# Attention ahead of two MoE layers: the mask added in PSUM by TensorE, one wide maximum and one wide sum per group, exps from PSUM, v sums on GpSimd, first weights loaded later

## Chip, core and metric

One core of one Trainium2 chip runs the whole program in one launch. The metric is device time in microseconds (us) of that core. The kernel before takes 1644.41 us (median of 3 runs, 1643.33 to 1644.82).

## What is computed

```python
# attention: B=2, H=8, S=768, D=64, block 32, window 16, nb = 24
k_sum = k.reshape(B, H, nb, block, D).max(axis=3)
v_sum = v.reshape(B, H, nb, block, D).mean(axis=3)
scores_l = where(|i - j| < 16, scale * q @ k.T, -1e9)          # scale = 1/8
scores_s = scale * q @ k_sum.T + log(32)
a = softmax(concat([scores_l, scores_s]))                      # sum + 1e-9 below the line
x = a @ concat([v, v_sum])                                     # -> [1536, 512]
# layer 1: 4 experts of 512 -> 1024 -> 512, all tokens, weighted by given probabilities
# layer 2: 8 experts of the same size, weighted by 8 rounds of row and column scaling of exp(logits)
```

All in float32 in and out.

## The kernel before

**Attention** runs over 8 pairs of heads (`pairs`), each in 3 groups (`NG`) of 4 query tiles of 64 rows (`GT`, `QT`). A query tile of both heads makes 128 rows; each row has 120 scores (`KX`): a band of 96 keys and the 24 block maxima of k. For a pair, `prep_k` transposes k and takes block maxima, `prep_q` transposes q into the block-diagonal tile `bd`, `reduce_v` sums v over 8 neighbouring rows (`vr`), `prep_v` finishes that sum with a matmul (`pv`, `vb`), and `spread_v` copies the 24 block means to the 24 last partitions of `vs`, whose first 96 partitions `load_vs` fills.

A group goes through `s1` (scores, mask, row maximum `nm`), `s1b` (exp, sum `sm`, reciprocal, and the multiply L404 on GpSimd), `s2` (transpose) and `s3` (times v). The loop at L445 has 24 + 4 passes; pass w, called **window w** here, issues s3 of group w-4, s2 of w-3, s1b of w-1, s1 of w, then, by w modulo 3, `prep_k` (0) or `prep_q` (1) of the next pair. `vslot` sets the sums of v at windows 0, 2, 4, 7, 10, 13, 16, 19; `prep_v` follows one window later, `spread_v` two. The schedule is manual: each engine and SyncE's DMA queue work in the order of the code.

At the end of each window `filler` issues work for the first layer: at window 3 the loads of the first weights (`load_w2(0)`, `load_w1(0)`, 512 KB each), from window 5 one piece per window of their split into a rounded high part (VectorE) and a rest (GpSimd, L128, and sums of quarters L178), from window 9 pieces that split x in the same way, from window 20 one step of the first products (`early`) per window.

**The MoE layers** follow as 48 units of weights (expert, quarter) times 2 halves of the tokens: TensorE makes products of the split parts (L487) and the second matmul (L562 to L564), the other engines split weights and add.

PSUM has 5 buffers of tag "m" (`ps`, `pa`, `po`, `pz`, `pm`) and 3 of tag "x".

## Time and profile before

| | |
|---|---|
| median of 3 runs | 1644.41 us (1643.33 to 1644.82) |
| the profiled execution | 1645.07 us, span 1643.4 us |
| busy, share of the span | PE 97%, PEld 87%, DVE 56%, ACT 36%, POOL 34% |
| chain that ended last | PE 90%, DVE 6%, ACT 1%, others 3% |

PE is TensorE's matmuls, PEld its weight loads, DVE is VectorE, ACT ScalarE, POOL GpSimd, SPq SyncE's DMA queue. The profile cuts the span in 40 slices of 41 us; attention fills about the first three. Windows are found on VectorE by their first instruction, L402 (it belongs to the sum of the group before).

### The profile page before, as it was taken

The page shows a single profiled execution, that of the slowest core. Times are in us where ns is not written, and L with a number is a line of the kernel's source. Part 1 is how long each engine was busy: PE and PEld are TensorE (multiplying, and loading weights), DVE is VectorE, ACT ScalarE, POOL GpSimd, SP SyncE. Part 2 cuts the span into 40 slices and gives each one's busy share as a digit, 9 for nine tenths or more (in the row PEclk, how much of TensorE's full clock was granted, in tenths as well). Part 3 has the DMA queues.
Part 4 walks back from the last instruction along what each step waited for, and adds up shares of the span by engine and source line. Part 5 has one row for each costly group of instructions (what it writes and reads, how often), then busy time and mean ns, then how long its engine had stood idle before and what let it go on. Part 6 is the DMA issues. An engine that isn't in the chain of part 4 may idle for free.

```text
span 1643.4 us, 21876 instructions
## 1 busy us (share of the span) xinstructions
PE 1599.0 (97%) x8419; PEld 1437.7 (87%) x8419; DVE 922.3 (56%) x1711; ACT 586.5 (36%) x1369; POOL 558.3 (34%) x642
## 2 busy tenths in 40 slices
PE   6879999999999999999999999999999999999999
PEld 5768899899899987889998998998998999989987
DVE  6886554554554556675555555545545545555555
ACT  4763233333333335433333333323323323323321
POOL 3644333323324333424324324324323323333330
PEclk9889999999999999999999999999999999999999
DMA  9831001001001100101100100100100100100102
GB/s 185 161 83 52 26 26 52 27 26 50 28 26 40 38 1 26 53 26 41 37 27 31 47 26 27 52 26 27 52 27 27 51 26 26 52 26 26 52 0 78
DMA packets 84520, 70.26 MB, mean 43 GB/s; under 512 B 36032, under 2 KB 69056, under 8 KB 84416
## 3 DMA queue, kind: packets, MB, share of 16 engines
q1 hardware_dynamic: 84416, 68.87, 14.5%
q8 instruction: 66, 1.08, 0.3%
q14 instruction: 38, 0.31, 0.1%
HBM read 64.53 MB, written 3.15 MB: 41 GB/s over the span
## 4 chain that ended last, share of the span: by engine, by line
PE 90%; DVE 6%; ACT 1%; issue 1%; DMA 1%; POOL 0%; SPq 0%; DVEq 0%; ACTq 0%
PE px L487 35%; PE pm L564 16%; PE pm L563 16%; PE pm L562 16%; PE pz L487 6%; ACT s L398 1%; DVE scr L211 1%; DVE vr L342 1%; DVE s L388 1%; DVE sm L402 1%; PE pg L622 0%; DVE hlo_b L500 0%; DVE c L516 0%; DMA vn<-in_v_dram 0%; DMA scr<-in_moe_w_dram 0%
## 5 line engine op out<-in xcount | busy, mean ns | idle before, releaser
L582 DVE SCALAR_TENSOR_TENSOR acc<-pm,pp,acc 128x512 f32<-128x512 f32 x359 | 269.6, 751 | 195.0 <-PE pm L564 193.3
L516 DVE TENSOR_TENSOR c<-pz,c 128x384 f32<-128x384 f32 x96 | 53.4, 557 | 317.9 <-PE pz L487 317.8
L128 POOL TENSOR_TENSOR w1lo_b<-scr,w1hi_b 128x512 fp32r<-128x512 f32 (+1 forms) x144 | 116.9, 830 | 317.0 <-ACT w1hi_b L125 309.4
L128 POOL TENSOR_TENSOR w1lo_a<-scr,w1hi_a 128x512 fp32r<-128x512 f32 (+1 forms) x144 | 118.4, 841 | 305.9 <-ACT w1hi_a L125 296.0
L521 ACT COPY c<-px 128x384 f32<-128x384 f32 x96 | 46.1, 480 | 436.6 <-PE px L487 436.5
L487 PE MATMUL px<-xhi,w1hi_a 128*128 128x384 f32 x576 | 195.5, 339 | 2.0 <-ACT c L521 1.0
L487 PE MATMUL px<-xhi,w1hi_b 128*128 128x384 f32 x576 | 194.1, 337 | 0.8 <-ACT c L530 0.8
L487 PE MATMUL px<-xlo,w1hi_a 128*128 128x384 f32 x576 | 193.8, 336 | 0.2 <-POOL xlo L128 0.2
L487 PE MATMUL px<-xhi,w1lo_a 128*128 128x384 f32 x576 | 193.8, 336 | 0.0
L487 PE MATMUL px<-xhi,w1lo_b 128*128 128x384 f32 x576 | 193.3, 336 | 0.0
L487 PE MATMUL px<-xlo,w1hi_b 128*128 128x384 f32 x576 | 193.3, 336 | 0.0
L582 DVE SCALAR_TENSOR_TENSOR acc<-pm,p,acc 128x512 f32<-128x512 f32 x180 | 135.0, 751 | 97.0 <-PE pm L564 97.0
L178 POOL TENSOR_TENSOR scr<-scr 128x256 f32<-128x256 f32 x188 | 137.6, 742 | 3.7
L516 DVE TENSOR_TENSOR c<-px,c 128x384 f32<-128x384 f32 x192 | 107.0, 557 | 46.6 <-PE px L487 46.5
L128 POOL TENSOR_TENSOR w2lo_a<-scr,w2hi_a 128x512 fp32r<-128x512 f32 x48 | 61.2, 1296 | 161.8 <-ACT w2hi_a L125 159.1
L128 POOL TENSOR_TENSOR w2lo_b<-scr,w2hi_b 128x512 fp32r<-128x512 f32 x48 | 60.9, 1292 | 161.0 <-ACT w2hi_b L125 161.0
L564 PE MATMUL pm<-w2hi_b,hlo_b 128*128 128x512 f32 x288 | 113.4, 394 | 2.3 <-DVE hlo_b L500 2.3
L495 ACT ACTIVATE hhi_a<-c 128x384 fp32r<-128x384 f32 x144 | 75.6, 525 | 112.0 <-DVE c L516 112.0
L562 PE MATMUL pm<-w2hi_b,hhi_b 128*128 128x512 f32 x288 | 112.8, 391 | 0.5 <-ACT hhi_b L495 0.5
L562 PE MATMUL pm<-w2hi_a,hhi_a 128*128 128x512 f32 x288 | 112.5, 391 | 0.7 <-ACT hhi_a L495 0.7
L564 PE MATMUL pm<-w2hi_a,hlo_a 128*128 128x512 f32 x288 | 112.6, 391 | 0.5 <-DVE hlo_a L500 0.5
L495 ACT ACTIVATE hhi_b<-c 128x384 fp32r<-128x384 f32 x144 | 75.6, 525 | 104.6 <-DVE c L516 104.5
(148 smaller groups left out, 3613.0 us busy)
## 6 DMA issues: line engine op xcount, KB each, us to landing
scr<-in_moe_w_dram SPq DMA_DIRECT2D x96, 512.0 KB, 4.6
vs<-in_v_dram SPq DMA_DIRECT2D x16, 240.0 KB, 4.8
kn<-in_k_dram SPq DMA_DIRECT2D x16, 192.0 KB, 4.0
qn<-in_q_dram SPq DMA_DIRECT2D x16, 192.0 KB, 4.4
vn<-in_v_dram SPq DMA_DIRECT2D x8, 384.0 KB, 3.8
out_dram<-acc SPq DMA_DIRECT2D x12, 256.0 KB, 2.0
vs<-vb SPq DMA_DIRECT2D x8, 144.0 KB
vs<-in_v_dram SPq DMA_DIRECT2D x32, 24.0 KB, 4.5
```

What stands on the lines that cost most here:

```text
L128: lo_eng.tensor_tensor(out=lo, in0=src, in1=hi.bitcast(F32), op=ALU.subtract)
L178: sum_eng.tensor_tensor(out=st[:, o], in0=x, in1=y, op=op)
L211: sum_eng.tensor_tensor(out=out, in0=x, in1=y, op=ALU.subtract)
L342: nc.vector.tensor_reduce(out=vr[i], in_=vn[i].rearrange("x h c d -> x h d c"), axis=AX.X, op=ALU.add)
L487: nc.tensor.matmul(pm, w[l][:, a, c, :], r[:, x, :], start=first and i == 0, stop=i == n - 1, skip_group_check=True,)
L495: nc.scalar.activation(out=hhi[:, f, t * HB:(t + 1) * HB], in_=c, func=AF.Relu)
L516: nc.vector.tensor_tensor(out=c, in0=pm, in1=c, op=ALU.add)
L521: nc.scalar.copy(out=c11, in_=px)
L562: nc.tensor.matmul(pm, hhi[:, c, ts], w["w2hi"][:, c, :], start=(c == 0), stop=False)
L563: nc.tensor.matmul(pm, hhi[:, c, ts], w["w2lo"][:, c, :], start=False, stop=False)
L564: nc.tensor.matmul(pm, hlo[:, c, ts], w["w2hi"][:, c, :], start=False, stop=(c == FC - 1))
L582: nc.vector.scalar_tensor_tensor(out=acc[T], in0=pm, scalar=scal, in1=acc[T], op0=ALU.mult, op1=ALU.add)
```

## The change

1. **Mask in PSUM** (`s1`): per group, two more matmuls with an identity as weights: the mask of 4 tiles (480 columns, fp32r, starting the accumulation), and the rest of log(32) after rounding (96 columns). The four score matmuls accumulate on them. The tables `maskr`, `maskl` and `identr` are made once, at the start, on VectorE.
2. **Scale in `prep_q`**: the copies of q become multiplications by 1/8.
3. **One wide maximum**: the four custom instructions at L388 (add mask, scale, write s, minimum), each with an accumulator read, become one TENSOR_REDUCE of 480 elements out of PSUM.
4. **Exps read PSUM** (`s1b`): scores no longer go through SBUF before the exp; the accumulator reads are gone, and one TENSOR_REDUCE of 480 elements on VectorE makes the sums.
5. **v sums on GpSimd** (`reduce_v`): one TENSOR_REDUCE of 1024 elements on VectorE becomes three additions on GpSimd, of 512, 256 and 128 elements.
6. **First weights later** (`filler`): loads at window 6 instead of 3; pieces from window 8 instead of 5, two of them at windows 8, 12 and 16.

```diff
@@ -48,8 +48,7 @@
     NG = NQ // GT
     GW = GT * QT
     SC = 1.0 / math.sqrt(D)
-    NEG = -1.0e9 / SC
-    FMAX = 3.0e38
+    NEG = -float(2 ** 30)
     BLK = S
     NB = NT // BLK
     TPB = BLK // P
@@ -224,6 +223,9 @@
 
     def attention(apool, filler):
         mask = apool.tile([P, 6, KX], F32, name="mask", bufs=1)
+        maskr = apool.tile([P, 6, KX], F32R, name="maskr", bufs=1)
+        maskl = apool.tile([P, GT, NS], F32R, name="maskl", bufs=1)
+        identr = apool.tile([P, P], F32R, name="identr", bufs=1)
         sel = apool.tile([NS * VQ, NS], F32, name="sel", bufs=1)
         bd = [apool.tile([P, NQ, 2, QT], F32, name=f"bd{i}", bufs=1) for i in range(2)]
         nsc = S // P
@@ -292,7 +294,13 @@
                         base=sgn * off + WIN,
                         channel_multiplier=-sgn,
                     )
-        nc.gpsimd.memset(mask[:, :, KW:KX], math.log(BLOCK) / SC)
+        nc.gpsimd.memset(mask[:, :, KW:KX], math.log(BLOCK))
+        nc.vector.tensor_copy(out=identr, in_=ident)
+        nc.vector.tensor_copy(out=maskr, in_=mask)
+        nc.vector.tensor_tensor(
+            out=maskl, in0=mask[:, 0:GT, KW:KX], in1=maskr[:, 0:GT, KW:KX].bitcast(F32),
+            op=ALU.subtract,
+        )
         for sgn, base in ((1, 0), (-1, VQ - 1)):
             nc.gpsimd.affine_select(
                 out=sel,
@@ -339,9 +347,13 @@
 
         def reduce_v(i):
             vr[i] = apool.tile([NS * VQ, 2, D], F32, name="vr", bufs=2)
-            nc.vector.tensor_reduce(
-                out=vr[i], in_=vn[i].rearrange("x h c d -> x h d c"), axis=AX.X, op=ALU.add
-            )
+            t, n = vn[i], BLOCK // VQ
+            while n > 1:
+                n //= 2
+                nc.gpsimd.tensor_tensor(
+                    out=t[:, :, 0:n] if n > 1 else vr[i][:, :, None, :],
+                    in0=t[:, :, 0:n], in1=t[:, :, n:2 * n], op=ALU.add,
+                )
 
         def prep_v(i):
             vb = apool.tile([KX, P], F32, name="vb", bufs=2)
@@ -364,46 +376,54 @@
                 pt = ps_x.tile([P, 512], F32, name="ptq", tag="x")
                 for c in range(nsc // 2):
                     nc.tensor.transpose(pt[:, c * P:(c + 1) * P], qn[i][:, j, c, :], ident)
-                copy = nc.scalar.copy if j else nc.vector.tensor_copy
+                scaled = nc.scalar.mul if j else nc.vector.tensor_scalar_mul
                 for r in range(2):
-                    copy(
-                        out=t[j * D:(j + 1) * D, :, j, r:QT:2],
-                        in_=pt[r * D:(r + 1) * D, 0:S // 2].rearrange(
+                    scaled(
+                        t[j * D:(j + 1) * D, :, j, r:QT:2],
+                        pt[r * D:(r + 1) * D, 0:S // 2].rearrange(
                             "x (t q) -> x t q", q=QT // 2
                         ),
+                        SC,
                     )
 
         def s1(i, g):
+
+
             ps = ps_m.tile([P, 512], F32, name="ps", tag="m")
+            pw = ps[:, 0:GT * KX]
+            wide = pw.rearrange("x (t k) -> x t k", k=KX)
+            nc.tensor.matmul(
+                pw, identr, maskr[:, g:g + GT].rearrange("x t k -> x (t k)"),
+                start=True, stop=False, skip_group_check=True,
+            )
+            nc.tensor.matmul(
+                wide[:, :, KW:KX], identr, maskl, start=False, stop=False, skip_group_check=True
+            )
             for tt in range(GT):
                 nc.tensor.matmul(
-                    ps[:, tt * KX:(tt + 1) * KX],
+                    wide[:, tt],
                     bd[i % 2][:, g * GT + tt].rearrange("x j q -> x (j q)"),
                     kw[i][:, g * GT + tt],
-                    start=True, stop=True,
-                )
+                    start=False, stop=True, skip_group_check=True,
+                )
+            nm = apool.tile([P, GT], F32, name="nm", bufs=4)
+            nc.vector.tensor_reduce(out=nm, in_=wide, axis=AX.X, op=ALU.max, negate=True)
+            return wide, nm
+
+        def s1b(ps, nm):
             s = apool.tile([P, GT, KX], F32, name="s", bufs=4)
-            nm = apool.tile([P, GT], F32, name="nm", bufs=4)
-            for tt in range(GT):
-                nc.vector.tensor_tensor_reduce(
-                    out=s[:, tt, :], in0=ps[:, tt * KX:(tt + 1) * KX], in1=mask[:, g + tt, :],
-                    scale=-SC, scalar=FMAX, op0=ALU.add, op1=ALU.min,
-                    accum_out=nm[:, tt:tt + 1],
-                )
-            return s, nm
-
-        def s1b(s, nm):
             sm = apool.tile([P, GT], F32, name="sm", bufs=5)
             for tt in range(GT):
                 nc.scalar.activation(
-                    out=s[:, tt, :], in_=s[:, tt, :], func=AF.Exp, scale=-1.0,
-                    bias=nm[:, tt:tt + 1], accum_out=sm[:, tt:tt + 1],
-                )
+                    out=s[:, tt, :], in_=ps[:, tt, :], func=AF.Exp, bias=nm[:, tt:tt + 1]
+                )
+            nc.vector.tensor_reduce(out=sm, in_=s, axis=AX.X, op=ALU.add)
             nc.vector.tensor_scalar_add(out=sm, in0=sm, scalar1=1e-9)
             nc.vector.reciprocal(out=sm, in_=sm)
             nc.gpsimd.tensor_tensor(
                 out=s, in0=s, in1=sm[:, :, None].to_broadcast([P, GT, KX]), op=ALU.mult
             )
+            return s
 
         def s2(s):
             pt = ps_m.tile([P, 512], F32, name="pa", tag="m")
@@ -449,9 +469,9 @@
             if g == 0 and 1 <= i < len(pairs):
                 load_vs(i)
             if 0 <= w - 3 < n:
-                av[w - 3] = s2(sv.pop(w - 3)[0])
+                av[w - 3] = s2(sv.pop(w - 3))
             if 0 <= w - 1 < n:
-                s1b(*sv[w - 1])
+                sv[w - 1] = s1b(*sv[w - 1])
             if w - 2 in vat:
                 spread_v(vat[w - 2])
             if w in vat:
@@ -710,7 +730,7 @@
 
         def filler(w, n):
             q = n // 4
-            if w == 3:
+            if w == q:
                 load_w2(0)
                 load_w1(0)
                 side["w"] = chain(
@@ -727,8 +747,10 @@
                 nc.vector.tensor_tensor(
                     out=p1, in0=dp, in1=dsum[:, :, None].to_broadcast([P, NTT, E1]), op=ALU.mult
                 )
-            if 5 <= w < 2 * q + 6:
+            if q + 2 <= w < 2 * q + 6:
                 next(side["w"], None)
+                if w % 4 == 0:
+                    next(side["w"], None)
             for i in range(3):
                 if w == (i + 1) * q + 3:
                     b, c = divmod(i, 2)
```

GpSimd's order around windows 7 to 10. Before, from window 9 (L404 is the softmax multiply, `w1lo_a` and L178 pieces of the weights, `xlo` pieces of x):

```order
L404 TENSOR_TENSOR s<-s,sm 128x480
L128 TENSOR_TENSOR w2lo_a<-scr,w2hi_a 128x512
L404 TENSOR_TENSOR s<-s,sm 128x480
L128 TENSOR_TENSOR w1lo_a<-scr,w1hi_a 128x512
L404 TENSOR_TENSOR s<-s,sm 128x480
L178 TENSOR_TENSOR scr<-scr 128x256 x2
L404 TENSOR_TENSOR s<-s,sm 128x480
L128 TENSOR_TENSOR w1lo_a<-scr,w1hi_a 128x256
L128 TENSOR_TENSOR xlo_82<-xfa,xhi_81 128x768
```

And now, from window 8 on (L423 is the multiply, L353 the sums of v):

```order
L423 TENSOR_TENSOR s<-s,sm 128x480
L127 TENSOR_TENSOR w2lo_a<-scr,w2hi_a 128x512 x2
L423 TENSOR_TENSOR s<-s,sm 128x480
L127 TENSOR_TENSOR w1lo_a<-scr,w1hi_a 128x512
L127 TENSOR_TENSOR xlo_82<-xfa,xhi_81 128x768
L423 TENSOR_TENSOR s<-s,sm 128x480
L353 TENSOR_TENSOR vn<-vn 96x2x256
L353 TENSOR_TENSOR vn<-vn 96x2x128
L353 TENSOR_TENSOR vr<-vn 96x128
L177 TENSOR_TENSOR scr<-scr 128x256 x2
L127 TENSOR_TENSOR xlo_82<-xfa,xhi_81 128x384
```

The pieces of the weights moved three windows down, onto those of x, and the three sums of v stand between a multiply and the pieces behind it.

SyncE's queue around the first weights. Before (L236 loads k, L356 is `spread_v` of pair 1, L253 loads v for the next sum, L245 q):

```order
L236 DMA kn<-in_k_dram 128x6x64 x2
L149 DMA scr<-in_moe_w_dram 128x2x512
L141 DMA scr<-in_moe_w_dram 128x4x256
L356 DMA vs<-vb 24x12x128
L253 DMA vn<-in_v_dram 96x2x512
L245 DMA qn<-in_q_dram 128x3x128 x2
```

Now, at window 6 (L368 is `spread_v`, here that of pair 2; L238 loads k, L255 v, L247 q):

```order
L368 DMA vs<-vb 24x12x128
L238 DMA kn<-in_k_dram 128x6x64 x2
L148 DMA scr<-in_moe_w_dram 128x2x512
L140 DMA scr<-in_moe_w_dram 128x4x256
L255 DMA vn<-in_v_dram 96x2x512
L247 DMA qn<-in_q_dram 128x3x128 x2
```

No `spread_v` stands close behind the weights now; the next v and q loads still do.

## Rows read from the trace of the kernel before

**Rows 1.** The page, part 1: busy us, share of the span, instructions of each engine.
```profile
PE 1599.0 (97%) x8419; PEld 1437.7 (87%) x8419; DVE 922.3 (56%) x1711; ACT 586.5 (36%) x1369; POOL 558.3 (34%) x642
```

**Rows 2.** Busy time by stretch: us, then PE, PEld, DVE, ACT, POOL busy (instructions), granted clock, DMA share, GB/s.
```profile
24.00:38.00 14.00, 9.10 (x103) 7.38 (x101) 11.97 (x55) 10.19 (x40) 5.17 (x5) 1.00 1.11 223
38.00:44.00 6.00, 5.13 (x36) 4.72 (x38) 1.37 (x6) 2.47 (x10) 1.46 (x2) 0.51 0.93 152
44.00:98.00 54.00, 43.31 (x453) 37.17 (x452) 50.62 (x189) 39.94 (x149) 32.62 (x30) 0.90 0.77 146
98.00:125.00 27.00, 21.11 (x194) 18.15 (x190) 20.86 (x66) 15.19 (x55) 13.91 (x10) 0.87 0.24 68
```

**Rows 3.** Timeline of TensorE around window 7: start us, us, engine, line, operation, out<-in, and in brackets the idle time before it with what ended it ("issue" is a wait that the profile has no releaser for).
```profile
38.87 1.12 PE L421 MATMUL po<-aT,vs 120*64 120x64 f32 x16 [4.48 <-issue]
...
51.27 1.05 PE L379 MATMUL ps<-kw,bd 128*128 128x120 f32 x8
```

**Rows 4.** Timeline of SyncE's DMA queue, windows 3 and 4.
```profile
28.98 1.30 SPq L149 DMA_DIRECT2D scr<-in_moe_w_dram  x1
30.33 0.47 SPq L141 DMA_DIRECT2D scr<-in_moe_w_dram  x1
30.90 0.83 SPq L356 DMA_DIRECT2D vs<-vb  x1
```

**Rows 5.** Timeline of VectorE: window 5's last instruction, the starts of windows 7, 10 and 17 (L402), and window 10 in between.
```profile
34.80 0.43 DVE L127 CAST w2hi_a<-scr 128x512 fp32r<-128x512 f32 x1 [0.86 <-DMA scr<-in_moe_w_dram]
...
43.25 0.17 DVE L402 TENSOR_SCALAR sm<-sm 128x4 f32<-128x4 f32 x1 [4.56 <-ACT s L398]
...
55.07 0.70 DVE L402 TENSOR_SCALAR sm<-sm 128x4 f32<-128x4 f32 x1
...
55.90 1.88 DVE L342 TENSOR_REDUCE vr<-vn 96x128 f32<-96x1024 f32 x1
57.70 0.27 DVE L388 CUSTOM_DVE_ANT_0 s<-ps,mask 128x120 f32<-128x120 f32 x1
...
58.51 1.12 DVE L369 COPY bd<-ptq 64x384 f32<-64x384 f32 x2
...
86.91 0.16 DVE L402 TENSOR_SCALAR sm<-sm 128x4 f32<-128x4 f32 x1
```

**Rows 6.** VectorE's groups by line, operation and shape: count, busy us, mean ns of one, idle us before them with its releaser.
```profile
L342 DVE TENSOR_REDUCE vr<-vn 96x128 f32<-96x1024 f32 x8 | 15.1, 1889 | 3.2 <-DMA vn<-in_v_dram 3.2
L402 DVE TENSOR_SCALAR sm<-sm 128x4 f32<-128x4 f32 x24 | 12.0, 499 | 11.8 <-ACT s L398 11.8
...
L331 DVE TENSOR_REDUCE ks<-pt 128x16 f32<-128x512 f32 x8 | 5.5, 687 | 2.5 <-PE pt L315 2.5
L127 DVE CAST xhi<-xfa 128x768 fp32r<-128x768 f32 x6 | 3.5, 577 | 0.0
L331 DVE TENSOR_REDUCE ks<-pt 128x8 f32<-128x256 f32 x8 | 3.3, 415 | 0.0
...
L642 DVE TENSOR_REDUCE mx<-lgt 128x1 f32<-128x96 f32 x1 | 0.3, 253 | 0.0
```

**Rows 7.** GpSimd's groups by line and shape, columns as in Rows 6.
```profile
L178 POOL TENSOR_TENSOR scr<-scr 128x256 f32<-128x256 f32 x188 | 137.6, 742 | 3.7
...
L128 POOL TENSOR_TENSOR w2lo_a<-scr,w2hi_a 128x512 fp32r<-128x512 f32 x48 | 61.2, 1296 | 161.8 <-ACT w2hi_a L125 159.1 <-DVE sm L402 1.5 <-DVE w2hi_a L127 1.3
...
L404 POOL TENSOR_TENSOR s<-s,sm 128x480 f32<-128x480 f32 x24 | 23.8, 991 | 38.5 <-DVE sm L403 33.3 <-ACT bd L369 2.4 <-ACT kw L327 1.5
...
L128 POOL TENSOR_TENSOR xlo<-xfa,xhi 128x768 fp32r<-128x768 f32 x6 | 11.5, 1911 | 2.9 <-DVE xhi L127 2.9
...
L128 POOL TENSOR_TENSOR xlo<-xfa,xhi 128x384 fp32r<-128x384 f32 x2 | 2.0, 1004 | 0.3 <-DVE xhi L127 0.3
```

**Rows 8.** ScalarE's groups, columns as in Rows 6.
```profile
L398 ACT ACTIVATE s<-s,nm 128x120 f32<-128x120 f32 x96 | 36.7, 386 | 17.6 <-DVE nm L388 17.6
...
L327 ACT COPY kw<-pt 128x96 f32<-128x96 f32 x8 | 1.9, 236 | 0.0
```

**Rows 9.** One of TensorE's groups with fp32r operands, and its wait for the sums of v, columns as in Rows 6.
```profile
L562 PE MATMUL pm<-w2hi_a,hhi_a 128*128 128x512 f32 x288 | 112.5, 391 | 0.7 <-ACT hhi_a L495 0.7
...
L349 PE MATMUL pv<-vr,sel 96*24 96x128 f32 x16 | 3.1, 278 | 9.5 <-DVE vr L342 9.5
```

**Rows 10.** The first 15 us, all engines (timeline).
```profile
6.59 0.69 DVE L331 TENSOR_REDUCE ks<-pt 128x16 f32<-128x512 f32 x1 [2.46 <-PE pt L315]
...
7.11 0.22 POOL L295 MEMSET mask<- 128x144 f32 x1
...
9.77 2.04 PE L379 MATMUL ps<-kw,bd 128*128 128x120 f32 x8 [1.52 <-DVE bd L369]
...
12.79 1.92 DVE L342 TENSOR_REDUCE vr<-vn 96x128 f32<-96x1024 f32 x1 [3.17 <-DMA vn<-in_v_dram]
...
14.74 0.28 DVE L388 CUSTOM_DVE_ANT_0 s<-ps,mask 128x120 f32<-128x120 f32 x1
```

**Rows 11.** DMA issues by line: KB each, median us from issue to landing.
```profile
vs<-in_v_dram SPq DMA_DIRECT2D x16, 240.0 KB, 4.8
```

**Rows 12.** Line 402 alone: duration ns minimum/median/maximum, first and last start.
```profile
L402 DVE TENSOR_SCALAR sm<-sm x24: 151/171/1770, 17.5 to 115.8; 128x4 f32<-128x4 f32 x24
```

**Rows 13.** Timeline of GpSimd, the instruction that ran when L402 of window 10 began.
```profile
54.77 0.97 POOL L128 TENSOR_TENSOR w1lo_a<-scr,w1hi_a 128x256 fp32r<-128x256 f32 x1 [1.60 <-DVE w1hi_a L127]
```

## Prediction

> **What bounds it now.** The busy times come first: TensorE 97% of the span [rows 1]. That is a mean over stages, so the next view is busy time by stretch. From 125 us on the kernel is a row of matmuls, and a change in attention only moves that row's start. Attention is another machine: from 44 to 98 us VectorE is busy 50.62 of 54.00 us, TensorE 43.31, ScalarE 39.94, GpSimd 32.62 [rows 2]. VectorE sets the pace there. The six microseconds before, 38 to 44, show the opposite: VectorE 1.37 of 6.00, TensorE's granted clock 0.51 [rows 2], so near its 1.2 GHz level. TensorE's timeline says why: the first matmul with vs of pair 1 starts at 38.87 after 4.48 us of waiting for something the profile cannot name [rows 3]. The DMA queue names it: two weight loads of 512 KB went out at 28.98 and 30.33, and the copy that completes vs went out behind them at 30.90 [rows 4]. VectorE pays for it at window 7: 4.56 us idle until 43.25 [rows 5]. So the change must be priced in three stretches of VectorE's time: A, to the start of window 7 (43.25); B, windows 7 to 16 (43.25 to 86.91, 43.7 us [rows 5]); C, the rest.
>
> **Prices.** Four L388 with their accumulator reads fill 57.70 to 58.51, 0.81 us; the sum of v fills 55.90 to 57.70, 1.80 us [rows 5]. The wide maximum reads 480 elements of PSUM: 512 take 687 ns and 256 take 415 [rows 6], so 1.06 ns per element and 653 ns; as neighbours overlap by some 80 ns (1.88 us long, next start after 1.80 [rows 5]) 0.57 us. The wide sum reads SBUF, which only two rows show: 96 elements in 253 ns, 1024 strided ones in 1889 [rows 6]. The first and the same slope give 661 ns, the second's rate gives 885; the new reduction is contiguous like the first, so 0.58 us, with 0.80 as the other end. A window thus pays 0.57 + 0.58 - 0.81 = **+0.34 us** on VectorE: wide is not cheaper here, since every element is now read twice. The gain has to come from the sum of v, **-1.80 us** in each of eight windows.
>
> On GpSimd the three additions of 512, 256 and 128 cost 1.30 + 0.74 + 0.46 us by its rows for 512 and 256 [rows 7], the last along the same line: 2.5 us for what VectorE did in 1.9.
>
> On ScalarE an exp with accumulator takes 386 ns and a 96-element copy out of PSUM 236 [rows 8]; the new exps lie between. Four used to start after the first L388 and now start after the whole maximum, so I take the delay from maximum to sum as unchanged: 0, within 0.5 us per window either way, and only where VectorE has nothing else to do.
>
> TensorE gets two fp32r matmuls per group, each below the 391 ns of a 512-column one [rows 9]: 24 x 0.78 = 18.7 us at most. I take 0, because scores run far ahead: those of window 10 start at 51.27 [rows 3] and are first read at 57.70 [rows 5]. If that lead went, 0.8 us per window would show. Scaling q by 1/8 rides on copies that were there: 0.
>
> **Stretch A.** The start gets later: maskr needs the finished mask, at 7.11 + 0.22 [rows 10]; its cast of 720 takes under 0.58 (768 take 577 ns [rows 6]) and maskl about 0.2, so the block maxima start at 8.1 instead of 6.59. Scores of window 0 move from 9.77 to 11.3, end some 2.7 us later with the masks, and the maximum ends at 14.6. Before, VectorE waited for v, summed it from 12.79 on, and did L388 from 14.74 to 15.55 [rows 10]: -1.0. Windows 2 and 4 lose the sum of v: -3.6. Windows 1 to 6 pay 6 x 0.34 = +2.0. The two pieces of weights that windows 5 and 6 held go, 0.4 us each, with 0.86 of waiting for their DMA [rows 5]: -1.7. The stall goes: -4.56. Together -8.9 on VectorE. What is late next is vs: without the weights its last copy can go out at 28.98, lands some 4.8 us later [rows 4, 11], and frees TensorE at about 33.5 where it was 38.87: only -5.4. The later one binds: **A = -5.5** (-3 to -8.9).
>
> The weights' loads now leave at about 34 us and have until window 8, near 41, before VectorE wants them; the first copy behind them that completes vs belongs to pair 3 and is issued at window 9, for window 13. That cover is the reason for 0 there; without it the stall comes back (below).
>
> **Stretch B.** VectorE: ten windows at +0.34 (+3.4), four sums of v gone (-7.2), two casts of weights that came in (+0.8): -3.0. Two things eat into it. First, L402, four elements long, has a median of 171 ns but a mean of 499 and a maximum of 1770 [rows 6, 12]: it waits for something, 0.33 us a time. That of window 10 began at 55.07 for 0.70 us [rows 5], and ended with the GpSimd instruction that had run since 54.77 for 0.97 [rows 13]. The Trainium skill, "SBUF — State Buffer", section "Who interferes with whom", has the rule: an op of VectorE in a two-port mode and a GpSimd op exclude each other for a whole instruction, while a tensor_reduce never contends. The trace agrees as far as L402's maximum is one xlo long (1.91 us [rows 7]); by that rule the two new reductions cost their own time, and L402 waits more as GpSimd fills. GpSimd's load in these ten windows is countable from the code's order: ten multiplies (9.9 us), four sums of v (10.0), three pieces of 512 (3.9), nine of 256 (6.7), four xlo of 768 (7.6), two of 384 (2.0): 40.1 us [rows 7] in a stretch that took 43.7. From 60% busy [rows 2] it goes to over 90%, so I raise the wait from 0.33 to 0.48 us: +1.5. Second, the sum of v now stands behind pieces on GpSimd, and TensorE's `pv` behind it, which waited 9.5 us in all already [rows 9]; mostly inside the lead, +1.0 taken. **B = -0.5**; no better than -3.6 (GpSimd full), +4 if its waits for VectorE's casts are not hidden.
>
> **Stretch C.** Seven windows at +0.34 (+2.4), one sum of v gone (-1.8): **C = +0.6** (-0.5 to +2.5). The MoE part is unchanged.
>
> Sum: -5.5 - 0.5 + 0.6 = -5.4 us from the profiled execution's 1645.07: 1639.7. That execution lies 0.66 above the median of the runs, so 1639.0.
>
> **Rivals.** (1) *GpSimd becomes the bound of B.* For: 40.1 of 43.7 us, and each piece there needs a cast by VectorE first. Against: a multiply is due only two windows later. If B takes 47 us instead of 43.2, the sum is -1.6: 1642.8, no difference to be measured. The Trainium skill, "GPSIMD Engine Reference", section "Engine selection", keeps elementwise work and reductions along the free axis on VectorE, GpSimd being about twice as slow; followed, it says that edit 5 should not pay.
>
> (2) *The stall only moves.* The load of v at window 7 must wait for GpSimd's last addition, and q for pair 4 is queued behind it and behind 1 MB. If these land late, window 10 waits as window 7 did: 4.5 us back, -0.9: 1643.5. Against: q had three windows, some 10 us.
>
> (3) *Slower: L402 waits for a whole GpSimd instruction.* Place: each group's sum, which the reciprocal, the multiply and the next maximum stand behind. If pieces pushed late by the sums of v always run when it comes, it waits half to all of 0.74 to 1.91 us, say half of an xlo, 0.95, in 24 windows: 22.8 us where the sum above holds 14 x 0.33 + 10 x 0.48 = 9.4, so +13.4: 1652. It decides by the mean of that instruction, 0.5 us before and 0.56 in the sum: from 0.56 + 5.4/24 = 0.79 on nothing is left of the gain, and from 0.92 it is slower by a measurable 3.3 us.
>
> (4) *More than forecast:* vs is not late, A reaches -8.9, B -3: 1633.
>
> **Chances.** 0.2% (3.3 us) is what a measurement of this kernel can tell from no change. Forecast 0.59, rival 1 0.12, rival 2 0.11, rival 3 0.11, rival 4 0.07. Faster is the forecast and rival 4: 0.66. Same: rivals 1 and 2, 0.23. Slower: 0.11. The range goes from 1633 (all of A and most of B) to 1646 (past rivals 1 and 2, short of both together); outside are most of rival 3 and half of rival 4.
>
> **What would show it.** Right: window 7 starts on VectorE near 37.5 us, TensorE has no 4 us wait for vs, the granted clock stays high there; the wide maximum takes about 0.65 us and the sum 0.66; windows 7 to 17 take 42 to 44 us with GpSimd over 85% busy. Wrong: a mean of L402's successor (L421) above 0.79 us, `pv` waiting several us for the sums of v, a VectorE wait for the weights at window 8, or a start later than 15 us on the first exp.

## The result: 17 us slower, where 5 us faster was forecast

The changed kernel takes 1661.71 us (median of 4 runs, 1659.96 to 1662.12) against 1644.62 for the kernel before beside it: ratio 1.0103, 95% interval 1.0085 to 1.0120. The forecast was 1639.0, range 1633 to 1646. The profiled execution has a span of 1660.4 us, before 1643.4. One execution of experiment e14 below took 8809.31 us where its six others took 1648.41 to 1650.95; it is left out of every number here.

### Where in the program

A window's start on VectorE is the first instruction after the sum of the exps, L402 before and L421 after. The first is window 1, the last window 24. Read from those rows of VectorE's timelines, in us:

| window | before | after | only the weights moved | after, v summed on VectorE |
|---|---|---|---|---|
| 1 | 17.46 | 19.13 | 17.59 | 19.13 |
| 4 | 28.21 | 32.72 | 29.31 | 31.54 |
| 7 | 43.25 | 45.67 | 38.94 | 42.90 |
| 11 | 60.01 | 62.28 | 56.02 | 60.80 |
| 12 | 63.94 | 70.43 | 59.66 | 64.93 |
| 17 | 86.91 | 97.54 | 81.22 | 90.12 |
| 24 | 115.84 | 134.01 | 110.15 | 121.72 |

(The last two columns are experiments, below.) By the prediction's stretches: A, to window 7, is +2.4 us (forecast -5.5); B, windows 7 to 17, takes 51.9 us for 43.7 (+8.2, forecast -0.5); C, windows 17 to 24, takes 36.5 for 28.9 (+7.5, forecast +0.6). The whole loss lies in the attention: from window 24 to the end of the span it is 1526.4 us for 1527.6. Busy time by stretch of the kernel after; columns as in [rows 2]:

```profile
26.00:45.67 19.67, 17.23 (x169) 15.03 (x170) 11.47 (x28) 10.97 (x32) 6.45 (x8) 0.83 0.83 169
45.67:97.54 51.87, 36.17 (x332) 32.25 (x332) 41.57 (x84) 25.65 (x73) 39.33 (x38) 0.84 0.64 135
97.54:134.01 36.47, 29.28 (x267) 25.51 (x268) 25.32 (x55) 17.55 (x51) 17.47 (x16) 0.84 0.40 94
134.01:218.00 83.99, 80.62 (x427) 71.82 (x426) 54.43 (x90) 30.55 (x65) 36.91 (x37) 0.99 0.11 38
```

VectorE no longer sets the pace: 41.57 us busy of 51.87 where it was 50.62 of 54.00 [rows 2]. TensorE is not full either, and its granted clock is 0.83 to 0.84 in these three stretches. From 134 us on the clock is back at 0.99: only the start of the row of matmuls has moved.

### Prices: as forecast, nearly

Groups of the kernel after over the first 200 us: count, busy us, mean ns of one, idle us before them with the releaser.

```profile
L417 ACT ACTIVATE s<-ps,nm 128x120 f32<-128x120 f32 x96 | 27.0, 371 | 4.1 <-DVE nm L410 4.0
L420 DVE TENSOR_REDUCE sm<-s 128x4 f32<-128x480 f32 x24 | 15.6, 648 | 22.2 <-ACT s L417 21.1 <-ACT wghl L763 1.0
L410 DVE TENSOR_REDUCE nm<-ps 128x4 f32<-128x480 f32 x24 | 15.5, 645 | 2.6 <-PE ps L403 2.2
L395 PE MATMUL ps<-maskr,identr 128*128 128x480 f32 x24 | 13.2, 548 | 0.0
L353 POOL TENSOR_TENSOR vn<-vn 96x512 f32<-96x512 f32 x8 | 10.5, 1313 | 2.4 <-DMA vn<-in_v_dram 2.4
L421 DVE TENSOR_SCALAR sm<-sm 128x4 f32<-128x4 f32 x24 | 8.6, 358 | 0.8
L353 POOL TENSOR_TENSOR vn<-vn 96x256 f32<-96x256 f32 x8 | 6.0, 744 | 0.6
L399 PE MATMUL ps<-maskl,identr 128*128 128x96 f32 x24 | 5.5, 229 | 0.0
L361 PE MATMUL pv<-vr,sel 96*24 96x128 f32 x16 | 4.3, 361 | 25.9 <-POOL vr L353 25.9
L353 POOL TENSOR_TENSOR vr<-vn 96x128 f32<-96x128 f32 x8 | 3.9, 490 | 0.6
```

The wide maximum takes 645 ns (forecast 653), the wide sum 648 (661), an exp 371, the three additions 1.31 + 0.74 + 0.49 us (1.30 + 0.74 + 0.46). L402's successor L421 has a mean of 358 ns, less than the 499 of before [rows 6]. One price was outside its bound: the mask matmul of 480 columns has a mean of 548 ns where less than 391 was taken (0.46 us for the one at 33.18, 0.75 for the one at 39.20, behind the wait shown next). What stands out is idle time: 25.9 us in front of `pv`, where it was 9.5 [rows 9], and 21.1 us in front of the sum of the exps, where L402 had 11.8 [rows 6].

### One wait, followed through

The kernel after, windows 4 to 6, timeline of all engines (start us, us, engine, line, operation, out<-in, and in brackets the idle time before it with what ended it):

```profile
32.16 0.69 PE L441 MATMUL po<-aT,vs 120*64 120x64 f32 x16
32.77 0.65 PE L431 MATMUL pa<-ident,s 128*120 128x128 f32 x4
...
33.24 0.99 POOL L423 TENSOR_TENSOR s<-s,sm 128x480 f32<-128x480 f32 x1 [6.11 <-DVE sm L422]
...
34.19 2.06 POOL L353 TENSOR_TENSOR vn<-vn 96x512 f32<-96x512 f32 x2
...
36.33 0.45 POOL L353 TENSOR_TENSOR vr<-vn 96x128 f32<-96x128 f32 x1
...
36.83 0.62 PE L361 MATMUL pv<-vr,sel 96*24 96x128 f32 x2 [2.20 <-POOL vr L353]
37.38 1.12 PE L441 MATMUL po<-aT,vs 120*64 120x64 f32 x16
...
38.44 1.11 PE L431 MATMUL pa<-ident,s 128*120 128x128 f32 x4
38.58 0.37 ACT L451 COPY xfa<-po 128x256 f32<-128x256 f32 x1 [3.30 <-PE po L441]
...
39.64 0.59 ACT L433 COPY aT<-pa 120x512 f32<-120x512 f32 x1 [0.69 <-PE pa L431]
...
40.12 1.12 ACT L417 ACTIVATE s<-ps,nm 128x120 f32<-128x120 f32 x4
...
41.34 0.65 DVE L420 TENSOR_REDUCE sm<-s 128x4 f32<-128x480 f32 x1 [3.56 <-ACT s L417]
...
42.03 0.17 DVE L421 TENSOR_SCALAR sm<-sm 128x4 f32<-128x4 f32 x1
```

Read it downwards. GpSimd's additions stand behind its multiply of s and end at 36.8. `pv` waits 2.20 us for them. Behind `pv` in TensorE's order stand po (s3) and pa (s2) of the next window. ScalarE's order has the copy of po and the copy of pa ahead of the exps, so the exps start at 40.12, although their scores had been in PSUM since 34.6 and their maximum was taken by 37.2. The sum on VectorE waits 3.56 us. So here the lead in the scores protects nothing: on ScalarE the exps stand behind copies that stand behind `pv`. It is not this window alone. ScalarE's waits for po at its copies, kernel after, first 200 us (who waits <- for whom: us in total, times, longest):

```profile
ACT xfa L451 <- PE po L441: 12.8, 8, 3.9
ACT scr L451 <- PE po L441: 12.6, 5, 6.3
```

These 25.4 us were 5.6 in the kernel before, while ScalarE's wait for the maximum fell from 17.6 to 4.0.

The rows of the timeline show a second price too: the same sixteen po matmuls take 0.69 us at 32.16 and 1.12 us at 37.38, the four pa 0.65 and 1.11. Clock by stretch around this wait and around that of window 11, same kernel:

```profile
32.00:34.50 2.50, 2.50 (x33) 2.20 (x30) 2.39 (x6) 2.13 (x6) 1.25 (x2) 1.00 1.04 214
34.50:37.30 2.80, 0.60 (x4) 0.15 (x2) 1.94 (x5) 0.78 (x4) 2.64 (x4) 0.90 0.08 13
37.30:40.80 3.50, 3.50 (x30) 3.23 (x30) 0.30 (x1) 1.53 (x5) 0.42 (x1) 0.59 0.86 228
...
60.00:64.00 4.00, 0.54 (x5) 0.35 (x4) 3.22 (x8) 1.22 (x5) 3.92 (x4) 1.00 0.01 3
64.00:71.00 7.00, 5.98 (x38) 5.40 (x39) 4.68 (x8) 2.05 (x7) 5.27 (x8) 0.51 0.81 180
```

TensorE stands still, and what it does next runs at a granted clock of 0.59 or 0.51, near the 1.2 GHz level. What this second price comes to over all windows no run separates.

### The profile page after: what moved, and what is told of

It reads as the page before. It is cut to its first block, busy times and chain, and to the rows that moved or that the text cites. A ratio compares the mean times of both kernels' runs of the same rounds, so it can differ in the third digit from the quotient of the medians.

```text
span 1660.4 us, 21746 instructions
## 1 busy us (share of the span) xinstructions
PE 1606.5 (97%) x8467; PEld 1445.9 (87%) x8467; DVE 922.7 (56%) x1562; ACT 576.3 (35%) x1273; POOL 580.3 (35%) x666
## 4 chain that ended last, share of the span: by engine, by line
PE 92%; DVE 4%; POOL 2%; issue 1%; ACT 1%; POOLq 0%; DVEq 0%; ACTq 0%
PE px L507 35%; PE pm L584 16%; PE pm L583 16%; PE pm L582 16%; PE pz L507 6%; POOL vn L353 1%; PE ps L403 1%; PE po L441 1%; DVE scr L210 1%; PE pa L431 1%; POOL s L423 0%; PE pg L642 0%; PE pt L323 0%; ACT s L417 0%; DVE sm L420 0%
## 5 line engine op out<-in xcount | busy, mean ns | idle before, releaser
L507 PEld LDWEIGHTS px<-xhi,w1hi_a 128*128 128x128 f32 x576 | 108.7, 189 | 5.8 <-DVE c L536 1.9
```

Of the source, the lines that this page charges most:

```text
L507: nc.tensor.matmul(pm, w[l][:, a, c, :], r[:, x, :], start=first and i == 0, stop=i == n - 1, skip_group_check=True,)
```

## The experiments

The experiments were timed in four sets (e1 to e4, e7 to e10, e11 to e14, e15 to e17), each beside runs of the kernel before. The median of these moves between 1644.1 and 1645.1 from set to set, so a microsecond between kernels of two sets says nothing.

### Which edit costs what

**e1**: the changed kernel, edit 5 undone.

```diff
-            t, n = vn[i], BLOCK // VQ
-            while n > 1:
-                ... three additions on nc.gpsimd
+            nc.vector.tensor_reduce(out=vr[i], in_=vn[i].rearrange("x h c d -> x h d c"), axis=AX.X, op=ALU.add)
```

> The changed kernel with only the sum of v put back on VectorE (one tensor_reduce of 1.9 us a pair, as before). Theory 1 (order): the loss of 17 us comes from pv on TensorE, which waits 2.2 to 5.4 us a pair for GpSimd's sum of v, with s3, s2 and so ScalarE's next exps queued behind it. Then the waits of pv on vr fall under 1 us a pair, VectorE is over 90% busy again between windows 7 and 17, and the time is 1643 to 1649 (the +0.34 us a window of the wide reductions is 8 us over 24 windows, the later start 2 to 3, and the stall of 4.6 us at window 7 goes the other way). Theory 2 (shared port): GpSimd's extra 2.5 us a pair hold up VectorE's operations; it also expects most of the time back, and is told from theory 1 by another run. Theory 3 (edits 1 to 4 themselves: the wide reductions, the mask matmuls on TensorE and the late start): 1656 to 1661, nearly nothing back.

Measured 1649.53 us, ratio to before 1.0031 (1.0020 to 1.0041). 12.2 us come back, 0.5 short of theory 1's range, so edit 5 costs 12 where it was to bring 12.6 on VectorE in the three stretches. VectorE is busy 45.38 of 47.22 us between windows 7 and 17, as theories 1 and 2 have it. The waits of pv do not fall under 1 us a pair: they are 12.6 us in all, of at most 3.4, now on VectorE's sum. But ScalarE's waits for po fall from 25.4 us to 2.0, and it waits for the maximum instead.

**e2**: the kernel before, with edit 5 and nothing else (the same lines, the other way round).

> The kernel before with nothing changed but the sum of v on GpSimd (three halving adds). Theory 1 (order): slower, 1651 to 1658; pv waits for vr 2 to 5 us in each pair, as in the changed kernel. Theory 2 (shared port): slower too, with the mean of the operation on L402 and of the other VectorE operations in windows 7 to 16 up by 30% or more. Theory 3: the sum of v is not the cause, and VectorE gives up 1.9 us for each of 8 pairs: 1635 to 1644.

Measured 1656.12 us, ratio 1.0067 (1.0054 to 1.0081): 11.0 us slower by itself, with 30.3 us of waiting at pv. L406, which is L402 there, has a mean of 404 ns, less than before, so VectorE's own short operations are not where the time is. There is a gain at first: window 1 starts at 15.30 us for 17.46, where VectorE had summed v from 12.79 on [rows 10]. It is gone by window 4 (30.07 for 28.21).

**e4**: the kernel before, with edit 6 and nothing else.

```diff
-            if w == 3:
+            if w == q:
...
-            if 5 <= w < 2 * q + 6:
+            if q + 2 <= w < 2 * q + 6:
                 next(side["w"], None)
+                if w % 4 == 0:
+                    next(side["w"], None)
```

> The kernel before with only the first weights' loads and their pieces moved (from window 3 to the first window of the second quarter, and the pieces from two windows after it). The stall of 4.6 us on VectorE in window 4 to 7 goes. If it is on the path, as the prediction had it, 1640 to 1642; if it only moves to the pieces that are now two to a window in every fourth window, 1643 to 1646; slower, 1647 or more, if the later weights hold up the first experts after the attention.

Measured 1640.54 us, ratio 0.9971 (0.9960 to 0.9983): 4.5 us faster. Window 7 starts at 38.94 for 43.25. The stall of 4.56 us [rows 5] was on the path and did not come back elsewhere: this term of the prediction was right.

What is left are edits 1 to 4: e1 has all but edit 5, e4 only edit 6, and 1649.53 - 1640.54 = +9.0 us. By the table above, 1.5 us of it is there at window 1, and from window 1 to 24 e1 takes 102.59 us for 92.56: 10.03 us in 23 windows, 0.44 a window where 0.34 was forecast. (The two make 11.6; the profiled executions, 1649.74 and 1639.63, are 10.1 apart, and e1 has 1.5 less from window 24 on.)

**e8**: e1 without the wide sum; each exp adds up its row again.

```diff
-                    out=s[:, tt, :], in_=ps[:, tt, :], func=AF.Exp, bias=nm[:, tt:tt + 1]
-                )
-            nc.vector.tensor_reduce(out=sm, in_=s, axis=AX.X, op=ALU.add)
+                    out=s[:, tt, :], in_=ps[:, tt, :], func=AF.Exp,
+                    bias=nm[:, tt:tt + 1], accum_out=sm[:, tt:tt + 1],
+                )
```

> The changed kernel with the sum of v on VectorE and without the wide sum: each exp adds up its own row as in the kernel before (ScalarE, about 0.19 us for the read of each sum), and still reads PSUM; mask in PSUM and the wide maximum stay. If VectorE's work is what prices edits 1 to 4 (0.44 us a window against the kernel before, of which the wide sum is 0.65 to 0.68), 15 us go from 1649.5: 1633 to 1638. Rival: four exps with sums take 1.55 us where they take 1.12 without, on the chain from the maximum to the reciprocal; then half of it comes back at most: 1641 to 1647.

Measured 1639.24 us, ratio 0.9968 (0.9955 to 0.9980): 10.3 us less than e1 (9.3 when each is taken against the kernel before of its own set), between the two expectations (the rival's 2.5 to 8.5, and 11.5 to 16.5). So of edits 1 to 4 the wide sum in place of the exps' own sums costs 9 to 10, and the mask in PSUM, the wide maximum and the exps out of PSUM together nothing or -1.3 us (1639.24 against e4's 1640.54). No run changes the mask matmuls alone, so their forecast of 0 is borne out but not shown: in 24 groups the maximum waited 0.4 us in all for scores (last row). Groups of this kernel:

```profile
L413 ACT ACTIVATE s<-ps,nm 128x120 f32<-128x120 f32 x96 | 33.6, 371 | 15.5 <-DVE nm L406 15.5
L413 ACT ACTIVATION_READ_ACCUMULATOR s<-ps,nm 128x1 f32 x96 | 20.6, 215 | 0.0
L406 DVE TENSOR_REDUCE nm<-ps 128x4 f32<-128x480 f32 x24 | 15.6, 651 | 0.8 <-PE ps L399 0.4
```

ScalarE takes 215 ns per accumulator read, and it had the room; VectorE, at 648 ns a group, had none.

**e9**: e8 with the two start copies on ScalarE.

```diff
-        nc.vector.tensor_copy(out=identr, in_=ident)
-        nc.vector.tensor_copy(out=maskr, in_=mask)
+        nc.scalar.copy(out=identr, in_=ident)
+        nc.scalar.copy(out=maskr, in_=mask)
```

> The kernel of the run before this one with the two copies that make the rounded identity and the rounded masks on ScalarE instead of VectorE, so that VectorE's first sums of k do not stand behind the masks. The first sum of the exps came 1.5 us later in the changed kernel than in the kernel before. If VectorE's order is what makes the start late, the first exps come 1.2 to 2.2 us earlier and the time falls by as much. Rival: GpSimd's mask selects (6.36 us after the change, 4.83 before) and TensorE's first mask matmul set the start whichever engine copies: within 0.5 us of the run before this one.

Measured 1639.22 us, ratio 0.9966 (0.9953 to 0.9978): no difference to e8. Window 1 starts 0.76 us earlier (17.68 for 18.44), and by window 17 that is gone (83.08 for 82.24). The rival was right on the time and wrong on the reason: the mask selects on GpSimd are back at 4.83 us, so it was a copy on VectorE that had drawn them out (last section).

### Is it the order on TensorE?

**e3**: the changed kernel, pv and its spread one window later.

```diff
+        pvat = {w + 1 + (i > 0): i for i, w in vslot.items()}
...
-            if w - 2 in vat:
-                spread_v(vat[w - 2])
+            if w - 1 in pvat:
+                spread_v(pvat[w - 1])
...
-            if w - 1 in vat:
-                prep_v(vat[w - 1])
+            if w in pvat:
+                prep_v(pvat[w])
```

> The changed kernel with pv and what goes before it on TensorE (the two pieces of the spread and the matmuls) issued one window later for all pairs but the first; GpSimd's work is the same. Theory 1 (order): the waits of pv on vr go from 3 to 5 us to under 1 us in pairs 1 to 7, and 8 to 13 us come back: 1648 to 1654. Theory 2 (shared port): GpSimd does the same work beside VectorE, so 1658 to 1662, with waits that only move from pv to VectorE. Theory 3: also 1658 to 1662.

Measured 1655.39 us, ratio 1.0064 (1.0051 to 1.0076): 6.3 us come back, between the theories. pv waits 1.7 us in all, as theory 1 says, but two new waits came: po for the reload of pair 1 ahead of window 7, now a window too late, and pa for GpSimd's multiply (10.4 us where the changed kernel has 0.7). The first, on the timeline of e3:

```profile
35.44 0.83 SPq L368 DMA_DIRECT2D vs<-vb  x1
...
40.28 1.12 PE L441 MATMUL po<-aT,vs 120*64 120x64 f32 x16 [3.47 <-issue]
```

Two of TensorE's waits in e3, for GpSimd (line waited for, us in total, times, longest):

```profile
PE pa L431 <- POOL s L423: 10.4, 8, 3.1
...
PE pv L361 <- POOL vr L353: 1.7, 2, 1.0
```

**e7**: the changed kernel, the sum and the load of v one window earlier instead, pv in its place.

```diff
+        rvat = {w - (i > 0): i for i, w in vslot.items()}
...
-            if w in vat:
-                reduce_v(vat[w])
-                if vat[w] + 1 < len(pairs):
-                    load_vn(vat[w] + 1)
+            if w in rvat:
+                reduce_v(rvat[w])
+                if rvat[w] + 1 < len(pairs):
+                    load_vn(rvat[w] + 1)
```

> The changed kernel with the sum of v on GpSimd and the load of v that follows it one window earlier for all pairs but the first; pv and the reload stay where they are. Moving pv instead gave back 6.3 us of the 12 that the sum of v costs, and brought a new stall of about 5 us at window 7, where po waited for the reload of pair 1, issued a window too late for its 4.8 us. Theory 1 (order, not load): here neither wait is left; pv waits under 1 us a pair, no stall at window 7, and the time is 1644 to 1650. Theory 2 (GpSimd's load: its 2.5 us a pair hold up its own multiplies and pieces wherever they are put): 1652 to 1658, with TensorE or ScalarE waiting for GpSimd's multiply of s instead.

Measured 1655.88 us, ratio 1.0070 (1.0057 to 1.0082), which is theory 2's range. pv waits 1.2 us in all, and still only 5.8 us come back. Part is again a reload (4.9 us at window 3 for vs, whose copy left at 24.69, behind the loads of v and q on SyncE's queue). The rest is GpSimd: pa waits 11.4 us in all for its multiply. Timeline of e7, window 10:

```profile
59.35 1.26 POOL L127 TENSOR_TENSOR w1lo_a<-scr,w1hi_a 128x512 fp32r<-128x512 f32 x1
...
59.67 2.73 DVE L421 TENSOR_SCALAR sm<-sm 128x4 f32<-128x4 f32 x1
...
60.58 1.79 POOL L127 TENSOR_TENSOR xlo<-xfa,xhi 128x768 fp32r<-128x768 f32 x1
...
62.78 0.99 POOL L423 TENSOR_TENSOR s<-s,sm 128x480 f32<-128x480 f32 x1 [0.41 <-DVE sm L422]
...
63.82 1.11 PE L431 MATMUL pa<-ident,s 128*120 128x128 f32 x4 [3.37 <-POOL s L423]
```

A four-element operation of VectorE takes 2.73 us, from inside one GpSimd instruction to the end of the next; the multiply that needs its result comes late, and TensorE waits 3.37 us. In e7 that operation has a mean of 759 ns.

**e12**: order without load. The sum of v stays on VectorE (e1), but last in its window; the load of the next v, which is issued behind it, moves with it.

```diff
-            if w in vat:
-                reduce_v(vat[w])
-                ...
             ...
             filler(w, n)
+            if w in vat:
+                reduce_v(vat[w])
+                ...
```

> The changed kernel with the sum of v on VectorE, but put behind all else that VectorE does in its window instead of ahead of the maximum. GpSimd has no more to do than before; only vr comes 2 to 4 us later for pv. Theory 1 (the wait of pv): pv waits 2 to 5 us a pair and 5 to 10 us are lost against 1649.5: 1654 to 1660. Theory 2 (GpSimd's load): 1648 to 1652.

Measured 1660.76 us, ratio 1.0100 (1.0086 to 1.0114): 0.8 above theory 1's range and 11.2 us lost against e1 by order alone, about as much as by the whole of edit 5. Of this, 1.8 us is there at window 1 (20.93 for 19.13). The later load of v is not what costs: no engine is seen to wait for it. The group of pv in e12, and that in e1:

```profile
L357 PE MATMUL pv<-vr,sel 96*24 96x128 f32 x16 | 4.0, 340 | 26.0 <-DVE vr L350 26.0
```

```profile
L357 PE MATMUL pv<-vr,sel 96*24 96x128 f32 x16 | 3.5, 301 | 12.6 <-DVE vr L350 12.6
```

26.0 us of waiting on VectorE do what 25.9 on GpSimd did in the changed kernel, and ScalarE's waits for po are back at 22.2 us. The wait of pv is a sufficient cause, whoever is late.

**e13**: the changed kernel, pv half a window later: behind the next window's po and pa, its reload in the window where it was.

```diff
             if w - 2 in vat:
+                prep_v(vat[w - 2])
                 spread_v(vat[w - 2])
...
-            if w - 1 in vat:
-                prep_v(vat[w - 1])
```

> The changed kernel with pv, its copy and its reload all issued in the same window in which the reload stood, so that on TensorE pv comes behind the next window's s3 and s2 (po and pa) instead of ahead of them; the reload keeps its window. Theory 1 (order): ScalarE's exps no longer stand behind pv; the waits for vr that are left cost less, and with no stall at window 7 the time is 1648 to 1654. Theory 2 (load): 1654 to 1659, as in the two runs that moved pv by a window or the sum by a window.

Measured 1652.67 us, ratio 1.0051 (1.0039 to 1.0064): 9.0 us come back, with GpSimd's work unchanged; window 7 starts at 41.67, pv waits 9.5 us in all and ScalarE 7.3 for po. Theory 1's range. But it ends 3.1 us above e1, although VectorE has eight sums of 1.87 us less to do.

### Is it GpSimd's load as well?

**e11**: e1, with the three additions done on GpSimd too, into memory that nothing reads. They also keep v's buffer from its next load until they are done, but no engine waits for v, and TensorE's wait for q is 1.0 us for 1.5 in e1 (2.1 in e15 below for 1.7 in e9).

```diff
+            if i:
+                ...
+                while n > 1:
+                    n //= 2
+                    nc.gpsimd.tensor_tensor(
+                        out=idle[:, :, 0:n], in0=t[:, :, 0:n], in1=t[:, :, n:2 * n], op=ALU.add,
+                    )
```

> The changed kernel with the sum of v on VectorE (1649.5 us by the run on that), and GpSimd doing the same three adds of v beside it for all pairs but the first, in the same places, into a spare tile that nothing reads. Pv waits for VectorE; only GpSimd's load and the free buffer of v, which its adds hold, are as in the changed kernel. Theory 1 (the wait of pv): 1648 to 1652. Theory 2 (GpSimd's load: its adds keep its own multiplies and pieces, and VectorE's port, busy): 1654 to 1661, with pa on TensorE waiting for GpSimd's multiply of s.

Measured 1653.64 us, ratio 1.0058 (1.0045 to 1.0072): 4.1 us for the load by itself, with pv's wait at 12.6 us as in e1. Between the theories: both hold, with order the larger.

**e10** and **e14**: e9, the best kernel, with the sum of v on GpSimd, once a window earlier (e7's edit) and once with pv behind po and pa (e13's).

> The kernel of the run before this one (sums by the exps, start tables on ScalarE, mask in PSUM, wide maximum, weights later) with the sum of v on GpSimd, one window earlier. Theory 1 (order): up to 1.9 us a pair less on VectorE: 2 to 10 us faster than the run before this one. Theory 2 (GpSimd's load): GpSimd's multiplies come late, 2 to 8 us slower than the run before this one.

> The best kernel so far (mask in PSUM, wide maximum, sums by the exps, weights later, start tables on ScalarE: 1639.2 us) with the sum of v on GpSimd and pv behind the next s3 and s2, as in the run before this one. Theory 1: the sum of v leaves VectorE at last without a wait, 1631 to 1637. Theory 2: GpSimd's load still costs, 1642 to 1649.

Measured 1650.89 us for e10, ratio 1.0038 (1.0024 to 1.0051), and 1649.39 for e14 (six executions), ratio 1.0029 (1.0017 to 1.0040): 11.7 and 10.2 us slower than e9, more than theory 2 had expected for e10 (up to 8) and at its upper end for e14 (1649). Theory 1 fails here: with VectorE's work cut, moving pv does not save the sum on GpSimd. e16 is the kernel of e14 again; the trace read below is its.

**e15**: e9 with the unread additions of e11. **e16**: e14 again. **e17**: e14 with one of the three additions; it leaves six of the eight rows of v out of each sum, so it serves for its time alone:

```diff
-            t, n = vn[i], BLOCK // VQ
-            while n > 1:
-                ...
+            nc.gpsimd.tensor_tensor(
+                out=vr[i][:, :, None, :], in0=vn[i][:, :, 0:1], in1=vn[i][:, :, 1:2], op=ALU.add,
+            )
```

> The best kernel so far (sums by the exps, sum of v on VectorE, start tables on ScalarE; 1639.2 us) with GpSimd's three adds beside it for all pairs but the first, into a spare tile that nothing reads. Pv waits for VectorE alone. If GpSimd's load in windows 7 to 17 is a floor of its own, as the four runs with the sum on GpSimd suggest, which all took 49.6 to 51.9 us there whatever VectorE had to do: 1647 to 1652, and windows 7 to 17 take over 48 us. If the load only matters through pv: 1638 to 1642, 43 to 45 us.

> The best kernel with the sum of v on GpSimd and pv behind the next s3 and s2, once more, for a trace of it: the time 1648 to 1651 as before. If GpSimd's load is the floor: windows 7 to 17 take 48 to 50 us with waits of pv under 12 us in all, and GpSimd's multiply of s or its pieces are what VectorE and TensorE wait for. If it is still the order: pv waits over 20 us in all.

> The same kernel with GpSimd's adds cut to one of the three (0.49 us a pair instead of 2.5; it adds two of the eight rows of v and leaves the other six out). VectorE has no sum of v either way. If GpSimd's load is the floor: nearly all of the 10.6 us come back and some of VectorE's 15 with them, 1632 to 1640. If something else holds these kernels at 1650 (the port, the reload's order, the later copy of pv): 1644 to 1650.

Measured 1645.41 us (ratio 1.0005, 0.9996 to 1.0014), 1650.04 (1.0031, 1.0019 to 1.0043) and 1638.23 (0.9963, 0.9949 to 0.9977). Windows 7 to 17 of the best kernel e9, of e15, e16 and e17, columns as in [rows 2]:

```profile
39.83:83.08 43.25, 35.81 (x358) 30.92 (x356) 40.10 (x78) 29.01 (x115) 29.82 (x28) 0.88 0.85 172
```

```profile
40.16:88.33 48.17, 37.93 (x359) 32.55 (x360) 43.89 (x78) 29.08 (x115) 38.40 (x38) 0.86 0.80 156
```

```profile
40.70:88.14 47.44, 35.49 (x360) 30.25 (x356) 37.98 (x74) 29.65 (x115) 37.98 (x37) 0.89 0.78 156
```

```profile
39.19:80.60 41.41, 33.15 (x360) 28.30 (x354) 34.68 (x74) 29.40 (x115) 31.98 (x31) 0.96 0.85 175
```

With GpSimd (the fifth busy time) at 38 us these ten windows take 47 to 48 us, whether VectorE (the third) has 43.89 or 37.98 to do. With GpSimd at 30 to 32 they take 41 to 43. In e15 pv waits 4.6 us in all, on VectorE. The additions without a reader cost 6.2 us there, so GpSimd's load is a cause of its own; the expected 1647 at least was 1.6 too high. What e16 loses beyond e15, 4.6 us, lies behind these windows: windows 17 to 24 take 33.66 us for 29.67, and pv waits 3.6 us there for GpSimd where it waits 0.2 for VectorE in e15. In e17 most of the load is gone and 11.8 us come back against e16.

e17 shows one thing more. It has no sum of v on VectorE and nearly none on GpSimd, and is only 1.0 us below e9 (1.7 when each is taken against the kernel before of its own set). VectorE's eight sums, some 15 us of work [rows 6], are worth no more than 1 to 2 us there, less what one addition a pair and the other place of pv may cost: VectorE is busy 34.68 of 41.41 us and waits for others.

The best full version is e9 or e8, 1639.2 us: it beats the kernel before by 0.3%, and the changed kernel by 22 us. Nearly all of that 0.3% is edit 6, which alone (e4) gives 1640.54.

## Why the prediction was wrong

Nearly the whole miss is edit 5. Its terms were -12.6 for VectorE's sums, +1.5 for L402 and +1.0 for `pv`, together -10.1; measured on top of the other edits it is +12.2 (e1). That is 22.3 of the 22.7 us between 1639.0 and 1661.71.

**The step that failed** is the second of the two that "eat into" stretch B: `pv`, it said, waits "mostly inside the lead, +1.0 taken". The lead meant was that of TensorE's scores, 5 us by [rows 3, 5]. It is real, and it is the wrong lead: the exps of the next group wait on ScalarE behind two copies, and these behind po and pa, which stand behind `pv`. The rows of windows 4 to 6 show no slack in that order. Its price is 9.0 us where 1.0 was taken (e13), and an equal wait made in another way costs 11.2 (e12). The prediction had the wait in its list of what would prove it wrong, took the 9.5 us of [rows 9] as mostly hidden, and did not follow who stands behind `pv` on TensorE and then on ScalarE.

**The gain that was taken in full**, -3.6, -7.2 and -1.8 us for the sums of v, was hardly there to be had. VectorE's busy time from 44 to 98 us had been read as the pace (50.62 of 54.00 [rows 2]), and each microsecond off it as a microsecond won. For the wide sum that holds to two thirds: 15.6 us of work more on VectorE cost 9 to 10 (e1 against e8). From there on it no longer holds: 15 us less are worth 1 to 2 (e17 against e9), and 1.0 where GpSimd makes its additions in both (e13 against e11, with pv at another place). No run takes the sums off VectorE in the kernel with the wide sum without GpSimd's additions.

**Rival 1**, GpSimd as the bound of B, was in the right place, at 1642.8 and a chance of 0.12. Its load was well counted (39.33 us busy, forecast 40.1), and e15 prices it at 6.2 us in the best kernel, e11 at 4.1 in e1; it forecast 47 us for B and 47 to 48 were seen in e15 and e16. The engine need not be full for that, at 38 of 47 to 48 us: in e16's ten windows its pieces wait 7.1 us for VectorE's casts, and its multiplies 4.8 for what VectorE makes of the sums. The Trainium skill, "GPSIMD Engine Reference", section "Engine selection", which keeps such reductions on VectorE, came out right: no run with the whole sum of v on GpSimd beat the same kernel with it on VectorE. (Its factor of about two is not what the rows show here: 2.54 us for 1.89.)

**Rival 3**, the only one that ended slower, had the right sign for a reason that did not happen: L421's mean fell to 358 ns where it needed 0.79 us. The mechanism exists: the mean is 759 ns in e7 and 921 in e10, where the sum of v comes a window earlier, 667 in e16, and once it is 2.73 us in the rows above. It does not follow from the shorter wait of pv alone, as e3 has 478 ns with 1.7 us of that wait; why it fell in the changed kernel is not shown.

**Right**: the stall at window 7 (-4.56 forecast; -4.5 in e4) and that it did not move (rival 2); the price of every new instruction but the mask matmul of 480 columns; and, as far as e8 shows it, the mask matmuls at 0. A small slip without weight: vs at 28.98 + 4.8 is 33.8, so -5.1 and not -5.4, and the 4.8 is that of another load of vs.

**Mis-sized**: a window's extra time, 0.44 us for 0.34. That it came out so near is partly luck. By work, the wide sum takes 0.69 and not 0.58, since the operation behind it reads it and there is no overlap of 80 ns to take off (41.34 to 42.03 in the timeline above). By time it costs 0.39 to 0.43 a window (e8), and the wide maximum in place of four L388, which was to bring 0.24 a window or 5.8 us, brought 0 to 1.3 with all that goes with it. And the start, forecast 1.0 us early, is 1.67 late at window 1. The mask was ready at 8.86 where 7.33 was taken (last section), and the first wide maximum runs from 14.87 to 15.53, so it ends when the four L388 had ended (14.74 + 0.81 [rows 5, 10]) where 14.6 was forecast; the first exp, at 16.39, is past the 15 us that the prediction had named as a sign of being wrong. Then VectorE waits 1.01 us for the next pair's k, and the sum of the exps, which ScalarE no longer makes, comes on VectorE only at 18.45, behind the copies of that k, and takes its 0.64.

Edit 5 costs 12.2 us on top of the other edits (e1) and 11.0 by itself (e2), so it hardly depends on them. What stays open is the inside of edit 5 beyond its two causes: order and load were each changed alone and each costs, 9 to 11 and 4 to 6 us, but e13 and e11 may share some of the same waits, so the two do not simply add to 12.2 plus the work that VectorE was spared.

## What to carry to other kernels

Before moving work off the engine that looks full, follow its result to the reader, and then read, engine by engine, what stands behind that reader in program order: a 2.5 us result that comes 2 us late held three engines here, and a lead of 5 us on another path did not help. A busy share of 90% priced work that was added better than work that was taken away: 15.6 us more on VectorE cost 9 to 10 us, 15 us less brought 1 to 2. An engine with waits between its pieces (GpSimd, 38 us of 48) can be a bound at 80%.
